# A six-layer cross network on one core: a load put behind another, one split eviction, a changed block order, and single-row-block evictions in the last layer

## The chip, the cores and the metric
The kernel runs on one core of one Trainium2 chip. The metric is the device time of one execution in microseconds (us); lower is better. The core has TensorE (PE) for matmuls into PSUM, VectorE (DVE) and ScalarE (ACT) for elementwise work, GpSimd (POOL), and SyncE (SP), which here only issues DMAs. ACT can issue DMAs too. Sixteen DMA engines serve all queues.

## The reference
Six layers of a cross network over 4096 rows of 416 values (26 x 16), with weights `ws` [6, 416, 416] and biases `bs` [6, 416], all in bf16:

```python
x = x0
for l in range(ws.shape[0]):
    x = x0 * (x @ ws[l] + bs[l]) + x
return x
```

## The kernel before
The activations are held transposed: 416 features are three blocks of 128 (m or k = 0, 1, 2) on the partitions and a remainder of 32. The 4096 rows are columns, in two halves (s = 0, 1) of 2048, each of four column groups (g = 0 to 3) of 512. The three blocks live in `XM` tiles [128, 3, 4096]. The remainder's four groups are packed into 128 partitions, 32 for each g (`XR`); `XRx` is the same with the groups' halves swapped, so that row matmuls of different groups can run side by side in PE's row quarters.

**Loads.** `load_x0t(s, g)` (line 76) is a transposing DMA that brings 512 rows of x0 into `XM[0]`; all eight are issued by SP in the order of g and s. `load_xrem` (line 81) brings the remainder as 64-byte segments, for s = 0 in two parts of 64 partitions (two column groups each); `x0_rem` (line 157) then turns a part into `XR` and `XRx` with three DVE steps: a 32x32 transpose, a reordering copy, and a copy to the swapped place. Line 99 issues the first part on ACT's queue, behind the first layer's weights (line 96), the biases and the remainder's weights. SP issues the transposes for g = 0 to 3 (lines 95, 103 to 105), the second remainder part (106), then the second half's loads and everything else. A DMA waits at its issue until the eighth DMA before it has landed, since there are eight completion semaphores.

**The first layer** (`first_layer`, line 219) goes half by half. For each block m it computes a column pair (two groups, h = 0 or 1) into one pair of PSUM banks; four pairs are used in rotation (`two_banks`, line 131). `full` issues three matmuls (k = 0 to 2) for one (m, group); `row` adds the remainder's product. The order of all this is written out by hand and is PE's order. `ew_main` (line 165) evicts a pair: ACT adds the bias (1 + bias in layer 0, which takes in the "+ x" of that layer) and writes 1024 columns as bf16 into a tile `t`; DVE multiplies by x0 (line 171). A pair can be written again when ACT has read it.

**Layers 1 to 4** (lines 300 to 327) use 32-column tiles of PE for the blocks and evict with two DVE steps, a multiply (line 173) and an add (174). At the end of layer 4, SP issues six transposing DMAs (`xl_dmat`, line 213) that turn the result into rows (`XLrows`).

**The last layer** (line 329 on) has the activations as stationary operand, so its result comes out in rows: 8 "quads" (q) of four 128-row blocks (g), each block 416 wide in one PSUM bank. The first six quads are evicted by pairs (`ew_pair`, line 360): ACT casts 832 columns, DVE multiplies by x0's rows (367) and adds `XLrows` (368), SP stores (369). The last two quads are evicted singly (`ew_single`, line 371): 416 columns each, where the add of a block (`close`, line 379) is issued behind the multiply of the next, so that DVE's neighbouring steps do not depend on each other. `t` tiles come from a pool of 6, output tiles `o` from a pool of 10 of [128, 2, 416].

Of the kernel before, what the change touches and what calls it, by code (L numbers as in the profile page):

```python
# [9 lines left out]
ACT = mybir.ActivationFunctionType  # L10
ALU = mybir.AluOpType
BF16 = mybir.dt.bfloat16
# [4 lines left out]
def kernel(  # L17
# [7 lines left out]
    nc = tc.nc  # L25
    B, D = x0.shape
    L = ws.shape[0]
    P = 128
    NK = 3
# [3 lines left out]
    NG = 4  # L33
    CW = 512
# [6 lines left out]
    tpool = ctx.enter_context(tc.tile_pool(name="tpool", bufs=6))  # L41
    opool = ctx.enter_context(tc.tile_pool(name="opool", bufs=10))
# [27 lines left out]
    def col0(s, g):  # L70
        return SW * s + CW * g
# [4 lines left out]
    def load_x0t(s, g):  # L76
        c0 = col0(s, g)
        nc.sync.dma_start_transpose(out=XM[0][:, :, c0:c0 + CW], in_=x0[c0:c0 + CW, 0:NK * P])  # L78


    def load_xrem(eng, s, p0, p1):
        with nc.allow_non_contiguous_dma(reason="64B row segments"):
            eng.dma_start(xrem[s][p0:p1], x0[SW * s + 16 * p0:SW * s + 16 * p1, NK * P:D].rearrange("(p t) r -> p t r", t=16))
# [12 lines left out]
    load_wm(nc.scalar, 0)  # L96
    nc.scalar.dma_start(bsb[:], bs[:, :])
    load_wr(nc.scalar, 0, 0, 1)
    load_xrem(nc.scalar, 0, 0, 64)
    nc.scalar.activation(dz[:, 1:2], dz[:, 0:1], ACT.Identity, bias=dz[:, 0:1], scale=1.0)  # L100
    for g in range(1, NG):
        nc.vector.tensor_copy(WR[32 * g:32 * g + 32, 0, :], WR[0:32, 0, :])  # L102
    load_x0t(0, 1)
    load_x0t(0, 2)
    load_x0t(0, 3)
    load_xrem(nc.sync, 0, 64, 128)
# [24 lines left out]
    def two_banks():  # L131
        i = 2 * (turn[0] % 4)
        turn[0] += 1
        return PS[:, i:i + 2, :]
# [22 lines left out]
    def x0_rem(s, p0, p1):  # L157
        nc.vector.transpose(out=xrt[s][p0:p1], in_=xrem[s][p0:p1])  # L158
        nc.vector.tensor_copy(XR[0][p0:p1, CW * s:CW * s + CW].rearrange("p (j t) -> p j t", t=16),
                              xrt[s][p0:p1].rearrange("p t j -> p j t"))  # L160
        for a in range(p0, p1, 64):
            nc.vector.tensor_copy(XRx[s][64 - a:128 - a, :], XR[0][a:a + 64, CW * s:CW * s + CW])


    def ew_main(l, s, m, h, pt, cur, nxt):
        c0 = col0(s, 2 * h)
        t = tpool.tile([P, 2 * CW], BF16, name="t")
        nc.scalar.activation(t[:], pt.rearrange("p a b -> p (a b)"), ACT.Identity, bias=bM[:, m, l:l + 1], scale=1.0)  # L168
        x0c = XM[0][:, m, c0:c0 + 2 * CW]
        if l == 0:  # L170
            nc.vector.tensor_tensor(out=nxt[:, m, c0:c0 + 2 * CW], in0=t[:], in1=x0c, op=ALU.mult)  # L171
            return
        nc.vector.tensor_tensor(out=t[:], in0=t[:], in1=x0c, op=ALU.mult)  # L173
        nc.vector.tensor_tensor(out=nxt[:, m, c0:c0 + 2 * CW], in0=t[:], in1=cur[:, m, c0:c0 + 2 * CW], op=ALU.add)  # L174

    def ew_rem(l, s, pr, curR, nxtR):
        tr = tpool.tile([P, 2 * CW], BF16, name="t")
        nc.scalar.activation(tr[:, 0:CW], pr, ACT.Identity, bias=bR[:, l:l + 1], scale=1.0)  # L178
        x0c = XR[0][:, CW * s:CW * s + CW]
        if l == 0:  # L180
            nc.vector.tensor_tensor(out=nxtR[:, CW * s:CW * s + CW], in0=tr[:, 0:CW], in1=x0c, op=ALU.mult)
            return
        nc.vector.tensor_tensor(out=tr[:, 0:CW], in0=tr[:, 0:CW], in1=x0c, op=ALU.mult)
        nc.vector.tensor_tensor(out=nxtR[:, CW * s:CW * s + CW], in0=tr[:, 0:CW], in1=curR[:, CW * s:CW * s + CW], op=ALU.add)
# [34 lines left out]
    def first_layer(s):  # L219
        cur, nxt = XM[0], XM[1]  # L220

        def full(pt, m, h, gl, first, last):
            c0 = col0(s, 2 * h + gl)
            for k in range(NK):
                nc.tensor.matmul(pt[:, gl, :], lhsT=WM[:, 0, k, 128 * m:128 * m + 128], rhs=cur[:, k, c0:c0 + CW],  # L225
                                 start=(first and k == 0), stop=(last and k == NK - 1), skip_group_check=True)

        def row(pt, m, h, swapped, first):
            for gl in range(2):
                r0 = 32 * ((2 * h + gl + 2 * swapped) % 4)  # L230
                src = XRx[s][r0:r0 + 32, :] if swapped else XR[0][r0:r0 + 32, CW * s:CW * s + CW]
                nc.tensor.matmul(pt[:, gl, :], lhsT=WR[r0:r0 + 32, 0, 128 * m:128 * m + 128], rhs=src,  # L232
                                 start=first, stop=(not first), tile_position=(r0, 0), skip_group_check=True)

        pa = [two_banks() for m in range(NK)]
        if s == 0:
            for gl in range(2):
                for m in range(NK):
                    full(pa[m], m, 0, gl, True, False)
        else:  # L240
            for m, gl in ((0, 0), (1, 0), (0, 1), (1, 1), (2, 0), (2, 1)):
                full(pa[m], m, 0, gl, True, False)
        pb = [two_banks()]
        row(pa[0], 0, 0, 0, False)
        row(pa[1], 1, 0, 1, False)
        row(pa[2], 2, 0, 0, False)
        if s == 1:
            row(pb[0], 0, 1, 0, True)
        if s == 0:
            x0_rem(0, 64, 128)  # L250
        for m in range(NK):
            ew_main(0, s, m, 0, pa[m], cur, nxt)
        for gl in range(2):
            full(pb[0], 0, 1, gl, s == 0, s == 1)
        if s == 1:
            ew_main(0, s, 0, 1, pb[0], cur, nxt)
        for m in range(1, NK):
            pb.append(two_banks())
            for gl in range(2):
                full(pb[m], m, 1, gl, True, False)  # L260
        if s == 0:
            row(pb[0], 0, 1, 0, False)
            row(pb[1], 1, 1, 0, False)
            row(pb[2], 2, 1, 1, False)
            x0_rem(1, 0, 128)
            for m in range(NK):
                ew_main(0, s, m, 1, pb[m], cur, nxt)
        else:
            row(pb[1], 1, 1, 0, False)
            row(pb[2], 2, 1, 1, False)  # L270
            rem_first(pb)
# [67 lines left out]
    def mm_q_full(q, py, gs, first):  # L339
        for g in gs:  # L340
            for k in range(NK):
                nc.tensor.matmul(py[g // 2][:, g % 2, 0:D], lhsT=cur[:, k, q_cols(q, g)], rhs=WM[:, l, k, :],  # L342
                                 start=(first and k == 0), stop=((not first) and k == NK - 1), skip_group_check=True)
# [13 lines left out]
                                 rhs=bLr[32 * g:32 * g + 1, :], start=False, stop=(q == begun and g < 2), tile_position=(32 * g, 0),  # L357
                                 skip_group_check=True)

    def ew_pair(q, h, py):  # L360
        s, i = quads[q]
        b0 = 16 * s + 8 * h + i
        t = tpool.tile([P, 2 * CW], BF16, name="t")
        tv = t[:, 0:2 * D].rearrange("p (a d) -> p a d", a=2)
        o = opool.tile([P, 2, D], BF16, name="o")
        nc.scalar.copy(tv, py[h][:, :, 0:D])  # L366
        nc.vector.tensor_tensor(out=tv, in0=tv, in1=X0rows[:, b0:b0 + 5:4, :], op=ALU.mult)  # L367
        nc.vector.tensor_tensor(out=o[:], in0=tv, in1=XLrows[:, b0:b0 + 5:4, :], op=ALU.add)  # L368
        nc.sync.dma_start(out_v[:, b0:b0 + 5:4, :], o[:])

    def ew_single(q, g, py):
        s, i = quads[q]
        b = 16 * s + 4 * g + i
        t = tpool.tile([P, 2 * CW], BF16, name="t")
        o = opool.tile([P, 2, D], BF16, name="o")
        nc.scalar.copy(t[:, 0:D], py[g // 2][:, g % 2, 0:D])  # L376
        nc.vector.tensor_tensor(out=t[:, 0:D], in0=t[:, 0:D], in1=X0rows[:, b, :], op=ALU.mult)  # L377

        def close():
            nc.vector.tensor_tensor(out=o[:, 0, :], in0=t[:, 0:D], in1=XLrows[:, b, :], op=ALU.add)  # L380
            nc.sync.dma_start(out_v[:, b, :], o[:, 0, :])

        return close

    for q in range(0, NQ - 2, 2):
        py = [new_pts()]
        mm_q_full(q, py[0], (0, 1), True)
        py.append(new_pts())
        mm_q_rows((q, q + 1), py, q)
        ew_pair(q, 0, py[0])  # L390
        mm_q_full(q, py[0], (2, 3), False)
        ew_pair(q, 1, py[0])
        for h in range(2):
            mm_q_full(q + 1, py[1], (2 * h, 2 * h + 1), False)
            ew_pair(q + 1, h, py[1])
    pending = []
    for q in range(NQ - 2, NQ):
        py = new_pts()
        mm_q_rows((q,), (py,), None)
        for g in range(NG):  # L400
            mm_q_full(q, py, (g,), False)
            close = ew_single(q, g, py)
            if pending:
                pending.pop()()
            pending.append(close)
    pending.pop()()


# [28 lines left out]
```

## Time and profile before

| | us |
|---|---|
| median of 3 runs | 131.99 (131.69 to 132.15) |
| the profiled execution | 131.1 |
| its span, first to last instruction | 129.3 |
| PE busy | 122.5 (95%) |
| DVE busy | 103.1 (80%) |
| ACT busy | 83.9 (65%) |
| PE waits for a transpose of x0, first layer | 0.4 |
| PE waits for an eviction by ACT, first layer | 0.2 |

Times in the views are counted from the span's start. "Busy" of an engine leaves out its sequencer's work such as issuing DMAs. A matmul's end is modelled and matmuls overlap, so a real gap of PE is longer than the wait that is listed: it is read from the distance of the starts. The 1.8 us of the execution outside the span are taken as fixed. In the timeline a line gives the start, the length, engine, line, operation, the tiles, the shape, the count of merged instructions, and in brackets the idle time before them with what ended it. `SPq` and `ACTq` are those engines' sequencers, here issuing DMAs; `PEld` is PE's weight load.

### The profile page before, as it was taken

What the parts mean: (1) busy time and instruction counts of PE and PEld (TensorE: products, weight loads), DVE (VectorE), ACT (ScalarE), POOL (GpSimd) and SP (SyncE); (2) the same over time, 40 slices, a digit from 0 to 9 for tenths busy, and PEclk for the clock granted to TensorE, in tenths of its full rate; (3) what the DMA queues carried; (4) which work ended last, traced back from release to release, by engine and by line L of the source; (5) the groups of instructions that cost most, each with busy time, mean ns of one, the idle gap of its engine ahead of it and who ended that gap; (6) DMA issues with size and microseconds to landing.
All of it is one profiled execution on the core that took longest, in us unless ns stands there. A gap on an engine that the chain in (4) does not pass through costs nothing.

```text
span 129.3 us, 3927 instructions
## 1 busy us (share of the span) xinstructions
PE 122.5 (95%) x1681; PEld 54.4 (42%) x1683; DVE 103.1 (80%) x186; ACT 83.9 (65%) x92; POOL 5.4 (4%) x18
## 2 busy tenths in 40 slices
PE   6989999999999999999999999999999999999940
PEld 2433343444544444434444544444444345544420
DVE  1163768547989898989898989898989999999990
ACT  0307567598757759756759666849665867567760
POOL 4110000300000000000000000000001200000000
PEclk9999999999999999999999999999999999999997
DMA  3999999999990000000000000000499899996553
GB/s 93 254 213 200 159 182 261 232 329 333 334 298 8 5 0 8 0 0 5 0 5 0 5 0 5 0 5 0 82 126 193 162 138 231 225 312 198 191 172 101
DMA packets 42021, 16.37 MB, mean 127 GB/s; under 512 B 30826, under 2 KB 42004, under 8 KB 42004
## 3 DMA queue, kind: packets, MB, share of 16 engines
q1 hardware_dynamic: 40504, 15.70, 54.5%
q10 hardware_dynamic: 1500, 0.42, 1.7%
q8 instruction: 13, 0.21, 0.7%
q14 instruction: 4, 0.03, 0.1%
HBM read 6.15 MB, written 3.41 MB: 74 GB/s over the span
## 4 chain that ended last, share of the span: by engine, by line
PE 88%; DMA 5%; DVE 1%; ACT 1%; SPq 1%; issue 1%; DVEq 0%
PE PS L190 49%; PE PS L342 12%; PE PS L225 10%; PE PS L196 5%; PE PS L207 5%; DMA XM<-in_x_dram 5%; PE PS L202 2%; PE PS L351 2%; PE PS L232 1%; PE PS L356 1%; SPq L78 1%; DVE t L377 1%; ACT t L168 1%; DVE o L380 1%; ACT t L376 0%
## 5 line engine op out<-in xcount | busy, mean ns | idle before, releaser
L168 ACT ACTIVATE t<-PS,bM 128x1024 bf16<-128x1024 f32 x60 | 62.1, 1114 | 30.8 <-PE PS L196 21.3
L190 PE MATMUL PS<-XM,WM 128*32 128x512 bf16 x1152 | 65.2, 379 | 0.0
L190 PEld LDWEIGHTS <-WM 128*32 128x32 bf16 x1152 | 29.7, 97 | 33.8 <-issue 5.1
L173 DVE TENSOR_TENSOR t<-t,XM 128x1024 bf16<-128x1024 bf16 x48 | 33.3, 694 | 4.2 <-ACT t L168 4.2
L174 DVE TENSOR_TENSOR XM<-t,XM 128x1024 bf16<-128x1024 bf16 x48 | 33.5, 699 | 3.1
L342 PE MATMUL PS<-WM,XM 128*128 128x416 bf16 x96 | 17.9, 340 | 0.0
L225 PE MATMUL PS<-XM,WM 128*128 128x512 bf16 x70 | 16.6, 379 | 0.7 <-DMA XM<-in_x_dram 0.4
L366 ACT CAST t<-PS 128x832 bf16<-128x832 f32 x12 | 10.2, 852 | 5.0 <-PE PS L342 2.5
L342 PEld LDWEIGHTS <-XM 128*128 128x128 bf16 x96 | 8.9, 98 | 8.7 <-issue 2.2
L225 PEld LDWEIGHTS <-WM 128*128 128x128 bf16 x72 | 6.8, 98 | 10.1 <-issue 2.7
L171 DVE TENSOR_TENSOR XM<-t,XM 128x1024 bf16<-128x1024 bf16 x12 | 7.9, 689 | 2.3 <-ACT t L168 2.1
L207 PE MATMUL PS<-XM,WM 128*32 128x512 bf16 x120 | 8.2, 379 | 0.0
L178 ACT ACTIVATE t<-PS,bR 128x512 bf16<-128x512 f32 x10 | 6.8, 694 | 1.4 <-PE PS L207 1.4
L368 DVE TENSOR_TENSOR o<-t,XLrows 128x832 bf16<-128x832 bf16 x12 | 7.1, 592 | 0.5
L196 PE MATMUL PS<-XR,WR 32*128 32x512 bf16 x96 | 7.3, 379 | 0.0
L367 DVE TENSOR_TENSOR t<-t,X0rows 128x832 bf16<-128x832 bf16 x12 | 7.0, 584 | 0.0
L158 DVE STREAM_TRANSPOSE xrt<-xrem 64x512 bf16<-64x512 bf16 (+1 forms) x3 | 2.1, 708 | 5.0 <-DMA xrem<-in_x_dram 5.0
L138 PE MATMUL PS<-warm 128*128 128x512 bf16 (+1 forms) x12 | 4.4, 536 | 1.2 <-DVE warm L89 1.2
L376 ACT CAST t<-PS 128x416 bf16<-128x416 f32 x8 | 4.0, 505 | 1.0 <-PE PS L342 0.8
L207 PEld LDWEIGHTS <-WM 128*32 128x32 bf16 x120 | 3.2, 97 | 3.2
L285 POOL COPY XLrows<-scrR 128x512 bf16<-128x512 bf16 x2 | 1.4, 704 | 74.1 <-DMA scrR<-XR 74.1
L102 DVE COPY WR<-WR 32x416 bf16<-32x416 bf16 x3 | 0.8, 259 | 4.5 <-DMA WR<-in_ws_dram 4.4
(39 smaller groups left out, 42.2 us busy)
## 6 DMA issues: line engine op xcount, KB each, us to landing
X0rows<-in_x_dram SPq DMA_DIRECT2D x4, 832.0 KB, 10.6
out_dram<-o SPq DMA_DIRECT2D x12, 208.0 KB, 2.5
WM<-in_ws_dram SPq DMA_DIRECT2D x5, 312.0 KB
out_dram<-o SPq DMA_DIRECT2D x8, 104.0 KB, 1.8
WR<-in_ws_dram SPq DMA_DIRECT2D x4, 130.0 KB, 5.3
WM<-in_ws_dram ACTq DMA_DIRECT2D x1, 312.0 KB, 3.3
XM<-in_x_dram SPq DMA_TRANSPOSE x8, 4.8
xrem<-in_x_dram SPq DMA_DIRECT2D x1, 128.0 KB
```

The lines of the kernel that those rows point to most:

```text
L168: nc.scalar.activation(t[:], pt.rearrange("p a b -> p (a b)"), ACT.Identity, bias=bM[:, m, l:l + 1], scale=1.0)
L171: nc.vector.tensor_tensor(out=nxt[:, m, c0:c0 + 2 * CW], in0=t[:], in1=x0c, op=ALU.mult)
L173: nc.vector.tensor_tensor(out=t[:], in0=t[:], in1=x0c, op=ALU.mult)
L174: nc.vector.tensor_tensor(out=nxt[:, m, c0:c0 + 2 * CW], in0=t[:], in1=cur[:, m, c0:c0 + 2 * CW], op=ALU.add)
L190: nc.tensor.matmul(pts[g // 2][32 * q:32 * q + 32, g % 2, :], lhsT=WM[:, l, k, 128 * m + 32 * q:128 * m + 32 * q + 32], rhs=cur[:, k, c0:c ...
L196: nc.tensor.matmul(pts[g // 2][:, g % 2, :], lhsT=WR[32 * g:32 * g + 32, l, 128 * m:128 * m + 128], rhs=curR[32 * g:32 * g + 32, CW * s:CW ...
L207: nc.tensor.matmul(pr[32 * g:32 * g + 32, :], lhsT=WM[:, l, k, NK * P:D], rhs=cur[:, k, c0:c0 + CW], start=False, stop=(k == NK - 1), tile ...
L225: nc.tensor.matmul(pt[:, gl, :], lhsT=WM[:, 0, k, 128 * m:128 * m + 128], rhs=cur[:, k, c0:c0 + CW], start=(first and k == 0), stop=(last ...
L342: nc.tensor.matmul(py[g // 2][:, g % 2, 0:D], lhsT=cur[:, k, q_cols(q, g)], rhs=WM[:, l, k, :], start=(first and k == 0), stop=((not first ...
L366: nc.scalar.copy(tv, py[h][:, :, 0:D])
L367: nc.vector.tensor_tensor(out=tv, in0=tv, in1=X0rows[:, b0:b0 + 5:4, :], op=ALU.mult)
L368: nc.vector.tensor_tensor(out=o[:], in0=tv, in1=XLrows[:, b0:b0 + 5:4, :], op=ALU.add)
```

## The change
The first part of the remainder is issued by SP, behind the transpose of the second column group, and no longer by ACT. In the first layer the row matmuls and the evictions of the first column pair go m = 0, 2, 1 in place of 0, 1, 2 (the one that reads `XRx` last); in the second half the blocks of the second column pair go (0,0), (1,0), (0,1), (1,1), (2,0), (2,1), where (m, g) were (0,0), (0,1), (1,0) and so on; one eviction, of m = 0 in the first half's second column pair, is split: ACT takes its first 512 columns and DVE the other 512, in one step that adds the bias and multiplies. In the last layer all 32 blocks are evicted singly, with each add behind the next block's multiply, `o` tiles hold one block (the pool is still of 10), and the very last store is issued by ACT.

```diff
     load_wr(nc.scalar, 0, 0, 1)
-    load_xrem(nc.scalar, 0, 0, 64)
     nc.scalar.activation(dz[:, 1:2], dz[:, 0:1], ACT.Identity, bias=dz[:, 0:1], scale=1.0)
...
     load_x0t(0, 1)
+    load_xrem(nc.sync, 0, 0, 64)
     load_x0t(0, 2)
     load_x0t(0, 3)
...
+    def split_first(s, m, h, pt, nxt):
+        c0 = col0(s, 2 * h)
+        t = tpool.tile([P, 2 * CW], BF16, name="t")
+        nc.scalar.activation(t[:, 0:CW], pt[:, 0, :], ACT.Identity, bias=bM[:, m, 0:1], scale=1.0)
+        nc.vector.scalar_tensor_tensor(out=nxt[:, m, c0 + CW:c0 + 2 * CW], in0=pt[:, 1, :], scalar=bM[:, m, 0:1],
+                                       in1=XM[0][:, m, c0 + CW:c0 + 2 * CW], op0=ALU.add, op1=ALU.mult)
+        nc.vector.tensor_tensor(out=nxt[:, m, c0:c0 + CW], in0=t[:, 0:CW], in1=XM[0][:, m, c0:c0 + CW], op=ALU.mult)
...
         row(pa[0], 0, 0, 0, False)
-        row(pa[1], 1, 0, 1, False)
-        row(pa[2], 2, 0, 0, False)
         if s == 1:
             row(pb[0], 0, 1, 0, True)
+        row(pa[2], 2, 0, 0, False)
+        row(pa[1], 1, 0, 1, False)
         if s == 0:
             x0_rem(0, 64, 128)
-        for m in range(NK):
+        for m in (0, 2, 1):
             ew_main(0, s, m, 0, pa[m], cur, nxt)
-        for gl in range(2):
-            full(pb[0], 0, 1, gl, s == 0, s == 1)
-        if s == 1:
-            ew_main(0, s, 0, 1, pb[0], cur, nxt)
-        for m in range(1, NK):
-            pb.append(two_banks())
-            for gl in range(2):
-                full(pb[m], m, 1, gl, True, False)
+        pb += [two_banks() for m in range(1, NK)]
+        for m, gl in ((0, 0), (0, 1), (1, 0), (1, 1), (2, 0), (2, 1)) if s == 0 else ((0, 0), (1, 0), (0, 1), (1, 1), (2, 0), (2, 1)):
+            full(pb[m], m, 1, gl, s == 0 or m > 0, s == 1 and m == 0)
+            if s == 1 and (m, gl) == (0, 1):
+                ew_main(0, s, 0, 1, pb[0], cur, nxt)
         if s == 0:
...
+            split_first(s, 0, 1, pb[0], nxt)
             x0_rem(1, 0, 128)
-            for m in range(NK):
+            for m in range(1, NK):
                 ew_main(0, s, m, 1, pb[m], cur, nxt)
...
-    def ew_pair(q, h, py):
...
     def ew_single(q, g, py):
...
-        o = opool.tile([P, 2, D], BF16, name="o")
+        o = opool.tile([P, D], BF16, name="o")
...
         def close():
-            nc.vector.tensor_tensor(out=o[:, 0, :], in0=t[:, 0:D], in1=XLrows[:, b, :], op=ALU.add)
-            nc.sync.dma_start(out_v[:, b, :], o[:, 0, :])
+            nc.vector.tensor_tensor(out=o[:], in0=t[:, 0:D], in1=XLrows[:, b, :], op=ALU.add)
+            (nc.scalar if (q, g) == (NQ - 1, NG - 1) else nc.sync).dma_start(out_v[:, b, :], o[:])
...
         mm_q_rows((q, q + 1), py, q)
-        ew_pair(q, 0, py[0])
-        mm_q_full(q, py[0], (2, 3), False)
-        ew_pair(q, 1, py[0])
-        for h in range(2):
-            mm_q_full(q + 1, py[1], (2 * h, 2 * h + 1), False)
-            ew_pair(q + 1, h, py[1])
-    pending = []
+        for g in range(2):
+            evict(q, g, py[0])
+        for a, g in ((0, 2), (0, 3), (1, 0), (1, 1), (1, 2), (1, 3)):
+            mm_q_full(q + a, py[a], (g,), False)
+            evict(q + a, g, py[a])
```

`evict` calls `ew_single` and then the `close` of the block before, as the last two quads' loop did before.

More of the change, by code (lines that the diff above doesn't have):

```diff
@@ L358, in mm_q_rows @@
                                  skip_group_check=True)
-    def ew_pair(q, h, py):
[L361 to L364, printed above, removed]
-        o = opool.tile([P, 2, D], BF16, name="o")
[L366 to L369, printed above, removed]
     def ew_single(q, g, py):
@@ L374, in ew_single @@
         t = tpool.tile([P, 2 * CW], BF16, name="t")
-        o = opool.tile([P, 2, D], BF16, name="o")
+        o = opool.tile([P, D], BF16, name="o")
         nc.scalar.copy(t[:, 0:D], py[g // 2][:, g % 2, 0:D])
@@ L379, in close, with evict @@
         def close():
-            nc.vector.tensor_tensor(out=o[:, 0, :], in0=t[:, 0:D], in1=XLrows[:, b, :], op=ALU.add)
-            nc.sync.dma_start(out_v[:, b, :], o[:, 0, :])
-        return close
+            nc.vector.tensor_tensor(out=o[:], in0=t[:, 0:D], in1=XLrows[:, b, :], op=ALU.add)
+            (nc.scalar if (q, g) == (NQ - 1, NG - 1) else nc.sync).dma_start(out_v[:, b, :], o[:])
+        return close
+    pending = []
+    def evict(q, g, py):
+        close = ew_single(q, g, py)
+        if pending:
+            pending.pop()()
+        pending.append(close)
     for q in range(0, NQ - 2, 2):
@@ L401 @@
             mm_q_full(q, py, (g,), False)
[L402 to L405, printed above, removed]
+            evict(q, g, py)
     pending.pop()()
```

## The prediction
> **What bounds the kernel now.** I read the 40 slices first, then the chain that ended last, then the timeline of the two ends of the span, where the change lies.
>
> The slices of the page, TensorE (PE) and the DMA engines:
> ```profile
> PE   6989999999999999999999999999999999999940
> ...
> DMA  3999999999990000000000000000499899996553
> ```
> A slice is 3.23 us. PE is full from slice 4 (about 10 us) to slice 38 (about 124 us), so time can only be won ahead of that, where PE has gaps and the DMA engines are full, and behind it, in the tail after the last matmul. The chain names the waits at the front (start, length, what):
> ```profile
> 2.17 5.92 DMA XM<-in_x_dram
> 8.09 0.04 issue
> 8.13 2.10 PE PS L225 x9
> ...
> 15.27 1.12 ACT t L168
> 16.40 0.04 issue
> 16.44 3.40 PE PS L225 x15
> ```
> Nine matmuls take 2.10 with a last one of 0.379, so they start 0.215 apart. The nine before these began at 5.64 and could have been followed at 7.58; the second transpose of x0 (call it T2, columns g=1) landed at 8.09 and PE went on at 8.13: 0.55 lost. At 16.44 PE waited for ScalarE (ACT) to free a PSUM pair: the three matmuls before began from 15.38 on, the next was due at 16.03; 0.4 lost. A third, smaller wait is seen only in the weight loads of the timeline:
> ```profile
> 2.27 0.63 ACTq L83 DMA_DIRECT2D xrem<-in_x_dram  x1
> ...
> 7.87 0.70 DVE L158 STREAM_TRANSPOSE xrt<-xrem 64x512 bf16<-64x512 bf16 x1 [0.77 <-DMA xrem<-in_x_dram]
> ...
> 11.51 2.90 PEld L225 LDWEIGHTS <-WM 128*128 128x128 bf16 x14 [0.27 <-issue]
> ...
> 11.92 0.71 DVE L158 STREAM_TRANSPOSE xrt<-xrem 64x512 bf16<-64x512 bf16 x1 [2.41 <-DMA xrem<-in_x_dram]
> ...
> 20.20 4.13 ACT L168 ACTIVATE t<-PS,bM 128x1024 bf16<-128x1024 f32 x4 [1.80 <-PE PS L232]
> 20.31 3.57 PEld L225 LDWEIGHTS <-WM 128*128 128x128 bf16 x18 [0.42 <-issue]
> ```
> The loads are idle 0.12 between neighbours but 0.27 ahead of 11.51: the fourth transpose (T4, issued 6.59, landing 4.88 later, at 11.47) held PE for 0.15. All that the front can give is therefore 0.55 + 0.15 + 0.4 = 1.1 us. The tail:
> ```profile
> 114.38 0.58 DVE L367 TENSOR_TENSOR t<-t,X0rows 128x832 bf16<-128x832 bf16 x1
> 115.00 0.59 DVE L368 TENSOR_TENSOR o<-t,XLrows 128x832 bf16<-128x832 bf16 x1
> 115.51 0.58 DVE L367 TENSOR_TENSOR t<-t,X0rows 128x832 bf16<-128x832 bf16 x1
> ...
> 122.86 2.09 ACT L376 CAST t<-PS 128x416 bf16<-128x416 f32 x4 [0.59 <-PE PS L342]
> ...
> 125.12 0.36 DVE L377 TENSOR_TENSOR t<-t,X0rows 128x416 bf16<-128x416 bf16 x1
> 125.40 0.65 DVE L380 TENSOR_TENSOR o<-t,XLrows 128x416 bf16<-128x416 bf16 x2
> ```
> The last add ends at 126.05; the last store is issued at 126.42, because SP is still busy until 126.33 issuing the store before. It lands at about 128.2 and the span ends at 129.3.
>
> **Part 1, the first remainder part behind T2 on SP.** It leaves ACT's queue, where its 0.63 hid nothing, and becomes SP's third issue. In the stretch 5.5 to 7.0 us the DMA view counts 1040 packets on ACT's queue (q10, 0.07 MB) beside 1170 on SP's (q1), at 47.9% and 88.3% of the sixteen engines. Without them T2 should land about 1.5 x 47.9/136.2 = 0.53 sooner, at about 7.55, and PE's wait of 0.55 goes. The next wait is T4's. PE reaches the row matmuls 0.55 sooner (10.16 to 9.61), needs T4 at 10.15 + 0.65 = 10.8, and T4 has not moved by the engines' work: the same packets must pass before it. So the 0.55 returns at T4, and what counts is T4's landing. Against it stands SP: an issue of 0.59 to 0.68 (rows of L83 on SP) is put ahead of T3 and T4, and every later load is behind it as well. Bounds: +0.7 if that issue counts in full; -0.7 if the mixing of two queues was what held T4 and both waits go. SP's transposes are issued in 1.38 at the shortest and 1.64 and 1.82 for T3 and T4, so most of the 0.68 meets slack, not all; I take **+0.2**. The remainder itself lands behind T2 (the second part landed 0.43 after T4), about 8.0; its three VectorE (DVE) steps took 7.87 to 9.51 = 1.64, so the direct copy is ready at 9.3, the swapped one at 9.65, against rows at 9.61 and (swapped, now last) 9.83. Were it 0.8 later, PE's wait for T4 would still hide it. [...]
>
> **Part 2, the split eviction.** Now the pair read by the second half's m=0 is freed by one ACT step of 1.114 (15.27 to 16.39). After, ACT reads 512 columns (L178: 0.69, to 15.96) and DVE the other 512. DVE is busy until 15.50 with three multiplies. The trace has no such DVE step: bounds are 0.42 (L181, 512 columns from SBUF) and 0.69 (ACT's read of 512 from PSUM); I take 0.69, since it reads fp32 from PSUM. Pair free at 15.54 + 0.69 = 16.23 instead of 16.39: **-0.15**; bounds -0.4 (all of the wait) and 0 (DVE late by another 0.2). DVE's step after it ends by 16.7, ahead of the remainder at 17.31.
>
> **Part 3, the block order.** In the first half nothing is reached: blocks keep their order, and m=1, now evicted third, is free at about 13.2, needed at 13.45. In the second half the order becomes (0,0), (1,0), (0,1)... Block (1,0) of the second column pair writes the PSUM pair that m=0 of the first used (four pairs in rotation). ACT's eviction of it runs 20.20 to 21.31. Before, PE comes there after two blocks, 20.31 + 2 x 0.65 = 21.6: hidden. After, it comes after one, at 20.97, and waits to 21.35: +0.38. Then m=1's eviction is third (20.20 + 3 x 1.0 + 0.1 = 23.32) and PE wants it at 21.35 + 3 x 0.65 = 23.29: +0.07. Sum **+0.45** (0.3 to 0.55; no reason for a gain, as no load was late here). What it buys, a later need of the eighth transpose, is not used: PE did not wait for that one.
>
> **Part 4, single evictions.** Twelve pairs become 24 singles. ACT: 24 x 0.505 - 12 x 0.852 = +1.9 us, beside PE: 8 singles need 4.3 of the 5.15 that PE takes. DVE: a pair starts every 1.13 (114.38 to 115.51), two singles take four starts 0.285 apart = 1.14: equal, +0.15 over the layer at most. DVE begins at 107.56 and 55 starts bring it to 123.26, where now it waits for ACT until 123.40; so nothing passes to the end. Output tiles: ten singles instead of ten pairs; the eleventh add comes at about 113.8, and the first store (issued 110.32 when SP is free of the transposes) landed 3.1 later with twice the bytes: 113.4. SP issues 31 stores of 0.34 to 0.37, one per 0.57. **0** (-0.1 to +0.2).
>
> **Part 5, the last store on ACT's queue.** ACT is idle after 124.95, so the store starts at 126.07 instead of 126.42: **-0.35**. Bounds: ACT's few issues took 0.32 to 0.66, so a slow one leaves 0; -0.45 with the wait trimmed.
>
> **Sum:** +0.2 - 0.15 + 0.45 + 0 - 0.35 = +0.15 on the profiled execution's 131.1 us (span 129.3). That execution lies 0.9 under the median 131.99 of the three timed runs; the difference is added to the median: **132.15 us**.
>
> **Rivals.**
> (a) The two queues held each other up, T4 comes 0.7 sooner, and part 1 is -0.7: sum -0.75, **131.25**. For it: q1's packets were fewest while q10 ran. Against: they were as few at 7.00 to 7.75 (167 GB/s), after q10 had ended.
> (b) Slower: the issue put ahead of T3 counts in full. After the third remainder SP needed 2.90 for the next transpose instead of about 1.4; half as large a part, 0.7. It decides from T4 landing after 11.7: sum +0.65, **132.65**.
> (c) Slower: DVE's fixed cost per instruction. A single lasts 0.368, half a pair's 0.584 is 0.292; only the overlap of neighbours brings the starts to 0.285. With 48 such steps ahead of the tail, a distance above 0.288 uses up the 0.14 of slack; at 0.31, a third of the way to 0.368, the end is 55 x 0.025 - 0.14 = 1.2 later: **133.35**. Against it: eight singles in the trace do keep 0.285. [...]
> (d) The store on ACT gains nothing, its first issue since the start being slow: +0.35, **132.5**.
>
> **Chances.** Forecast 0.41, (a) 0.25, (b) 0.16, (c) 0.07, (d) 0.11. 0.3%, about what a measurement of this kernel can tell, is 0.4 us: faster 0.25, same 0.41, slower 0.34. The range takes in (a), (b), (d): 131.1 to 132.9; the forecast's own is 131.6 to 132.4.
>
> **What would show it.** Right: no PE wait near 7.6, a new one of 0.7 or more ahead of T4's block; ACT still ending PE's wait near 16.3; a new wait of 0.4 one block into the second half's second column pair; DVE starts 0.285 apart; last store issued within 0.1 of the last add. Wrong: T4 landing before 11.0 or after 12.0, or DVE idle for an output tile near 114.

## The result, and the profile after

The changed kernel takes 132.61 us (median of 22 runs, 131.95 to 133.47); the kernel before took 131.93 beside it (22 runs, 131.43 to 132.88). The ratio is 1.0049 [1.0031, 1.0067], +0.65 us: slower by more than 0.3%. The forecast was 132.15, "same", with 131.6 to 132.4 as its own range and 131.1 to 132.9 as the whole one. The time is outside the first and inside the second, and is that of the slower rival (b), 132.65.

The profiled execution of after took 132.79 (span 131.0), near its median. The one of before, 131.1, lies 0.8 below its median and below the fastest of the 22 runs, 131.43. So the two traces stand 1.69 apart where the medians stand 0.68 apart, and not every difference between them belongs to the change.

The slices of after, TensorE and the DMA engines (3.27 us each):
```profile
span 131.0 us, 4011 instructions
...
PE   6998999999999999999999999999999999999920
...
DMA  3999999999992000000000000000597999964665
```
PE's 8 at the front has moved from the third slice, where T2's wait was, to the fourth, where T4's is now; and the loads at the front reach into the thirteenth slice. The timeline of after, SyncE's issues and PE at the front:
```profile
0.73 4.17 SPq L78 DMA_TRANSPOSE XM<-in_x_dram  x2
...
4.95 0.67 SPq L83 DMA_DIRECT2D xrem<-in_x_dram  x1
...
5.67 3.60 SPq L78 DMA_TRANSPOSE XM<-in_x_dram  x2
...
5.86 0.61 PE L138 MATMUL PS<-warm 128*128 128x512 bf16 x1
...
6.25 4.35 PE L234 MATMUL PS<-XM,WM 128*128 128x512 bf16 x18
...
11.08 0.82 PE L234 MATMUL PS<-XM,WM 128*128 128x512 bf16 x3
...
12.23 3.40 PE L234 MATMUL PS<-XM,WM 128*128 128x512 bf16 x15 [0.34 <-DMA XM<-in_x_dram]
```
In before the x18 were two lines of x9 with T2 between them. T2 landed at 6.99 (8.09 before), well ahead of PE. The x18 alone does not show that the change took the wait away, for PE also begins 0.61 later than in before. There the last filler matmul, on a constant tile ahead of the first layer, takes 0.39 and not 0.61:
```profile
5.41 0.39 PE L138 MATMUL PS<-warm 128*128 128x512 bf16 x1
```
Five of the other traces, with the remainder on ACT as before, begin at 6.25 or 6.26 and do not wait for T2 either, though it lands at 7.90 to 8.09. So the 0.55 at T2 that part 1 aims at belongs to executions in which PE begins early, as in the profiled one of before; part 1 alone, below, begins at 5.55 and has no such wait.

Three matmuls last 0.65 by their starts, so the row of 11.08 could have gone on at 11.73; T4, landing at 12.19 (11.47 before), held it to 12.23. That is 0.72 behind before's 11.51.

The next stretch of after: ACT's and DVE's halves of the split eviction, PE, and PE's weight loads in the second half:
```profile
15.98 0.69 ACT L180 ACTIVATE t<-PS,bM 128x512 bf16<-128x512 f32 x1 [1.89 <-PE PS L241]
...
16.10 4.06 PE L234 MATMUL PS<-XM,WM 128*128 128x512 bf16 x18
...
16.63 0.74 DVE L181 SCALAR_TENSOR_TENSOR XM<-PS,bM,XM 128x512 bf16<-128x512 f32 x1
...
21.72 1.82 PEld L234 LDWEIGHTS <-WM 128*128 128x128 bf16 x9 [0.41 <-issue]
...
23.73 0.96 PEld L234 LDWEIGHTS <-WM 128*128 128x128 bf16 x5 [0.19 <-issue]
```
The eighteen matmuls at 16.10 run through: where before PE stood 0.4 for ACT, it stands for nothing, although DVE reads its half until 17.37: the block at 16.75 writes only the bank that ACT has read by 16.67. In the second half the weight loads stop ahead of 21.72 and 23.73, where ACT has just freed a pair: 0.29 and 0.07 of PE. With 0.13 for row matmuls that wait for the remainder, the sum is +0.72 - 0.40 + 0.13 + 0.29 + 0.07 = +0.81; layer 1 begins at 27.18 against 26.36 (0.82). The last layer's first matmul is 0.81 later too, so the layers between hand it on whole.

The tail of after, from the timeline (stores are `SPq` and `ACTq` lines):
```profile
116.94 1.58 SPq L377 DMA_DIRECT2D out_dram<-o  x1
```
```profile
126.26 0.65 DVE L376 TENSOR_TENSOR o<-t,XLrows 128x416 bf16<-128x416 bf16 x2
126.94 0.37 ACTq L377 DMA_DIRECT2D out_dram<-o  x1
```
```profile
126.84 1.87 SPq L377 DMA_DIRECT2D out_dram<-o  x4
...
128.31 0.40 SPq L377 DMA_DIRECT2D out_dram<-o  x1
```
The last add ends at 126.91 and ACT issues its store 0.03 later, as forecast. But SP is behind: three of its stores go out after that one, the last at 128.31, 1.68 after its own add, and it lands last, at 130.05. From last add to last landing it is 3.14, against 2.14 before.

SP's lag also held DVE once, as the chain that ended last shows:
```profile
115.98 3.33 DMA out_dram<-o
...
119.40 0.28 DVE o L376
```
The add at 119.40 waited for an output tile whose store, issued at 115.98, landed at 119.31. DVE started it 0.48 after the step before instead of 0.285, so 0.2 later. In before DVE waits 0.15 for ACT at 123.40; that slack took up most of the 0.2, and the last add comes 0.05 later than the 0.81 by which the last layer begins later.

### The profile page after: what moved, and what is told of

It is laid out like the page before. It is cut to its first block, busy times and chain, and to the rows that moved or that the text cites. A ratio compares the mean times of both kernels' runs of the same rounds, so it can differ in the third digit from the quotient of the medians.

```text
span 131.0 us, 4011 instructions
## 1 busy us (share of the span) xinstructions
PE 123.6 (94%) x1683; PEld 54.7 (42%) x1683; DVE 104.2 (80%) x211; ACT 84.8 (65%) x104; POOL 5.5 (4%) x18
## 5 line engine op out<-in xcount | busy, mean ns | idle before, releaser
L168 ACT ACTIVATE t<-PS,bM 128x1024 bf16<-128x1024 f32 x59 | 61.1, 1114 | 30.3 <-PE PS L205 21.3
L174 DVE TENSOR_TENSOR XM<-t,XM 128x1024 bf16<-128x1024 bf16 x48 | 33.5, 699 | 3.1
L372 ACT CAST t<-PS 128x416 bf16<-128x416 f32 x32 | 15.6, 506 | 4.6 <-PE PS L363 1.8
L376 DVE TENSOR_TENSOR o<-t,XLrows 128x416 bf16<-128x416 bf16 x32 | 11.7, 367 | 0.1
L373 DVE TENSOR_TENSOR t<-t,X0rows 128x416 bf16<-128x416 bf16 x32 | 11.7, 367 | 0.0
L171 DVE TENSOR_TENSOR XM<-t,XM 128x1024 bf16<-128x1024 bf16 x11 | 7.3, 689 | 1.8 <-ACT t L168 1.6
L138 PE MATMUL PS<-warm 128*128 128x512 bf16 (+1 forms) x12 | 5.1, 594 | 1.2 <-DVE warm L89 1.2
L193 DVE TENSOR_TENSOR XR<-t,XR 128x512 bf16<-128x512 bf16 x8 | 3.4, 426 | 0.7
```

Source lines behind the costliest of these rows:

```text
L376: nc.vector.tensor_tensor(out=o[:], in0=t[:, 0:D], in1=XLrows[:, b, :], op=ALU.add)
```

## The experiments

All were timed against the kernel before in five rounds. A time given behind a ratio is the ratio less one, times the median of the kernel before beside it (131.38 to 131.96). The experiments take the parts singly first. Five kept traces have the first layer of before: that of before, those of parts 4 and 5, of part 5 alone and of the joint stores, and that of the last run below. They tell what is chance in it.

**Part 1 alone.**
```diff
-    load_xrem(nc.scalar, 0, 0, 64)
...
     load_x0t(0, 1)
+    load_xrem(nc.sync, 0, 0, 64)
```


> Only part 1: the first remainder part is issued by SP behind the second transpose. Theory (read from the changed kernel's trace): the fourth transpose lands about 0.7 us later and PE waits for it, so +0.7 us (ratio 1.005). Rival, the forecast's step: +0.2. Rival of mixed queues: -0.7. In the profile: the weight load that waits for the fourth transpose begins near 12.2 by the theory, near 11.7 by the forecast, near 10.9 by the third.

Measured: 1.0032 [1.0011, 1.0053], +0.42. PE in its timeline:
```profile
5.55 4.04 PE L225 MATMUL PS<-XM,WM 128*128 128x512 bf16 x18
...
10.06 0.82 PE L225 MATMUL PS<-XM,WM 128*128 128x512 bf16 x3
11.82 3.40 PE L225 MATMUL PS<-XM,WM 128*128 128x512 bf16 x14 [0.94 <-DMA XM<-in_x_dram]
...
16.75 3.40 PE L225 MATMUL PS<-XM,WM 128*128 128x512 bf16 x15 [0.24 <-ACT t L168]
...
21.71 3.40 PE L225 MATMUL PS<-XM,WM 128*128 128x512 bf16 x14 [0.27 <-DMA XM<-in_x_dram]
```
T2's wait is gone, T4's grew to 1.1 (10.71 to 11.82), ACT's stayed, and there is a wait for T8 (the eighth transpose) that the profiled execution of before did not have: T8 landed at 21.67 (20.83 before), 0.4 lost. This second wait cannot be put down to part 1. In the five traces with before's first layer T8 landed at 20.83 to 21.48, and in three of them PE waited for it, 0.14 to 0.58. What T4 costs is clearer. The block behind it begins at 11.66 to 12.23 in the three traces with the load on SP (after, this one, parts 1 to 3), and at 11.30 to 11.89 in the nine traces in which that load, SP's other loads and the block order of the first half are as in before. The means lie 0.37 apart, about what was timed.

**Part 2 alone.**
```diff
+            split_first(s, 0, 1, pb[0], nxt)
             x0_rem(1, 0, 128)
-            for m in range(NK):
+            for m in range(1, NK):
                 ew_main(0, s, m, 1, pb[m], cur, nxt)
```


> Only part 2: the one eviction split over ACT and DVE. Theory: the next block needs only the bank that ACT frees, so the whole wait of 0.4 us near 16.4 goes: -0.4. Rival, the forecast's step: DVE's half, 0.69 long and behind three multiplies, ends the wait, -0.15. In the profile: PE goes on at about 16.03 by the theory, at 16.27 by the forecast.

Measured: 0.9998 [0.9975, 1.0022], 0.0 us. PE in its timeline:
```profile
15.34 4.06 PE L233 MATMUL PS<-XM,WM 128*128 128x512 bf16 x18
...
19.94 0.82 PE L233 MATMUL PS<-XM,WM 128*128 128x512 bf16 x3
21.12 3.40 PE L233 MATMUL PS<-XM,WM 128*128 128x512 bf16 x14 [0.36 <-DMA XM<-in_x_dram]
```
The wait for ACT is gone in full: x18 at 15.34, no break at 16. At 20.59 PE then wants T8, which landed at 21.08: 0.53 lost, more than was won. The transpose that PE "did not wait for" in the profiled execution of before was simply there 0.1 before PE came (20.83 against 20.96); in other executions it is not.

**Part 3 alone.**
```diff
-        row(pa[1], 1, 0, 1, False)
-        row(pa[2], 2, 0, 0, False)
         if s == 1:
             row(pb[0], 0, 1, 0, True)
+        row(pa[2], 2, 0, 0, False)
+        row(pa[1], 1, 0, 1, False)
...
-        for m in range(NK):
+        for m in (0, 2, 1):
...
+        for m, gl in ((0, 0), (0, 1), (1, 0), (1, 1), (2, 0), (2, 1)) if s == 0 else ((0, 0), (1, 0), (0, 1), (1, 1), (2, 0), (2, 1)):
```


> Only part 3: rows and evictions in the order m = 0, 2, 1 and the changed block order of the second half. Theory and forecast agree: +0.45, a wait of 0.38 for ACT ahead of the second block and 0.07 ahead of the fifth. Rival: the rows' order of the first half gives something back, so 0.2 or less.

Measured: 1.0051 [1.0035, 1.0068], +0.67. PE in its timeline:
```profile
10.92 2.76 PE L225 MATMUL PS<-XM,WM 128*128 128x512 bf16 x11
13.99 1.46 PE L225 MATMUL PS<-XM,WM 128*128 128x512 bf16 x6 [0.31 <-ACT t L168]
...
16.97 3.40 PE L225 MATMUL PS<-XM,WM 128*128 128x512 bf16 x15 [0.24 <-ACT t L168]
...
21.90 3.47 PE L225 MATMUL PS<-XM,WM 128*128 128x512 bf16 x14 [0.23 <-ACT t L168]
```
Three waits for ACT. The one at 21.90 is the forecast 0.38 (measured 0.40). The one at 13.99 (0.47) was not forecast: m=1, evicted third, is wanted in the first half too.

**Parts 4 and 5 alone** (the whole last layer of after), and **part 5 alone:**
```diff
-            nc.sync.dma_start(out_v[:, b, :], o[:, 0, :])
+            (nc.scalar if (q, g) == (NQ - 1, NG - 1) else nc.sync).dma_start(out_v[:, b, :], o[:, 0, :])
```


> Only the last layer: all blocks evicted singly, last store on ACT. Theory: SP, which starts late behind the transposes and issues a store each 0.49 us, does not catch up with an add each 0.57, so its last store goes out 1 us or more after the add: +0.3 to +1.0. Rival, the forecast's step: SP catches up and the last store on ACT gives -0.35. In the profile: the last SP store starts within 0.3 of its add by the rival, over 0.8 behind it by the theory.

> Only part 5: the very last store issued by ACT, the last layer still in pairs but for its last two quads. Theory and forecast: the store starts at its add instead of 0.37 later, -0.35. Rival: a first issue on ACT after so long is slow, 0.

Measured: parts 4 and 5 1.0003 [0.998, 1.0026], 0.0; part 5 1.002 [1.0003, 1.0037], +0.26. The tail of part 5 alone, and the wait for its landing:
```profile
125.62 0.65 DVE L380 TENSOR_TENSOR o<-t,XLrows 128x416 bf16<-128x416 bf16 x2
126.31 0.38 ACTq L381 DMA_DIRECT2D out_dram<-o  x1
```
```profile
SPq L432 <- DMA out_dram<-o: 1.9, 1, 1.9
```
The add ends at 126.28 and the store is issued 0.03 later, 0.12 behind SP's store of the block before. It landed at 128.43, 2.12 after its issue, where in before the last store took 1.77. From add to landing it is 2.15 against 2.14: what the issue gains, the transfer loses. SP waits 1.9 for the landing, against 1.4 in before.

**Pairs stored jointly in the last layer of after,** one store for two blocks in the first six quads (19 issues on SP rather than 31):
```diff
+            if q >= NQ - 2:
+                (nc.scalar if (q, g) == (NQ - 1, NG - 1) else nc.sync).dma_start(out_v[:, b, :], o[:, 0, :])
+            elif e:
+                nc.sync.dma_start(out_v[:, b - 4:b + 1:4, :], o[:])
```


> Parts 4 and 5, but the 24 blocks of the first six quads, still evicted singly, are stored two by two, so that SP issues 19 stores and not 31. Parts 4 and 5 alone gave 0.0. Theory: what took the gain of part 5 is SP's queue of stores, so here SP keeps up and -0.35 is left. Rival: single evictions cost DVE or ACT what part 5 gains, so 0.0 as before.

Measured: 1.0000 [0.9977, 1.0023]. In its trace SP is no longer behind at the end (its last store goes out at 126.52, ahead of the last add's end at 126.61); in that of parts 4 and 5 it is:
```profile
125.28 1.85 SPq L370 DMA_DIRECT2D out_dram<-o  x4
126.14 0.41 ACTq L370 DMA_DIRECT2D out_dram<-o  x1
```
SP's last store goes out at 126.74, 0.9 after its own add (125.82). Taking SP's lag away changes nothing that the timing can tell: the lag is real, and its price in the usual execution lies within the interval, some 0.3 us.

**Parts 1 to 3** with before's last layer:


> Parts 1, 2 and 3 with the last layer as before. Alone they gave +0.4, 0.0 and +0.7. Theory: they overlap. Part 1 brings the rows of the first half forward and so hides m=1's third eviction (0.47 of part 3), and part 3 hides the wait for the eighth transpose that ate part 2's gain; so +0.5 to +0.7, all of the change's +0.65. Rival: the parts add up to +1.1, and the last layer gives 0.4 back.

Measured: 1.0035 [1.0017, 1.0054], +0.46, which with the last layer's 0.0 agrees with the whole change's +0.65 [0.41, 0.88] within the intervals. PE in its timeline:
```profile
11.66 3.46 PE L233 MATMUL PS<-XM,WM 128*128 128x512 bf16 x15 [0.25 <-DMA XM<-in_x_dram]
...
15.58 4.06 PE L233 MATMUL PS<-XM,WM 128*128 128x512 bf16 x18
...
20.44 4.41 PE L233 MATMUL PS<-XM,WM 128*128 128x512 bf16 x18
```
The 0.47 of part 3 in the first half is down to 0.06: x15 lasts 3.46 where 3.40 is free of waits, because ACT begins earlier (the row matmuls start at 10.05 here, at 10.38 in part 3 alone) while PE, held 0.4 by T4 (11.24 to 11.66), comes to that pair no earlier. The second-half wait for ACT stays, hidden in a merged line (4.41 against 4.06, 0.35).

**The order without its wait.** If part 3's loss is the pair that ACT frees too late, splitting that eviction as well should leave the gain: T8 is needed one block later, and ACT frees the first bank in 0.69 instead of 1.11. No load is moved; rows and evictions keep 0, 1, 2.
```diff
         for m in range(NK):
-            ew_main(0, s, m, 0, pa[m], cur, nxt)
+            if (s, m) == (1, 0):
+                split_first(s, m, 0, pa[m], nxt)
+            else:
+                ew_main(0, s, m, 0, pa[m], cur, nxt)
```
This with part 2, the second half's block order, and part 5; then the same without part 5; then with a third split (first half, m = 0, first pair) and the new block order in both halves:


> A version that should beat both: before, with part 2, part 5, the changed block order of the second half alone (rows and evictions still in the order m = 0, 1, 2), and a second split eviction, of m=0 in the second half's first column pair. Theory: the block that part 3 made wait needs only one bank, which ACT's half frees at 0.69 instead of 1.11, so the wait of 0.38 goes, the eighth transpose is needed later, and both waits of 0.4 are saved: -0.4 - 0.35 = -0.75. Rival: DVE's steps come later for it and the next wait takes most of it: -0.35, part 5 alone.

> The version with two split evictions, without part 5. Part 5 alone gave +0.26, since its store shares the DMA engines with the one issued 0.12 before it and lands 2.15 after its add, as it did on SP (2.14). Theory: this version, -0.37 with part 5, comes to -0.4 to -0.6. Rival: part 5's +0.26 was chance, so -0.37 as before.

> As the version with two splits without part 5, and the first half gets the same block order, with a third split (m=0 of its first column pair, DVE's half ahead of the second remainder part). Theory: the fourth transpose is needed 0.65 later, so its wait of 0.15 to 0.4 goes as well: another -0.2 to -0.35, -0.6 to -0.9 in all. Rival: the next wait (the eighth transpose, landing 20.5 to 21.5) takes it, no gain over two splits.

Measured: 0.9972 [0.9956, 0.9988], -0.37; without part 5 0.9966 [0.9945, 0.9987], -0.45; three splits 0.9966 [0.9940, 0.9992], -0.45. PE of the second of them:
```profile
10.60 4.10 PE L233 MATMUL PS<-XM,WM 128*128 128x512 bf16 x17
...
15.16 4.06 PE L233 MATMUL PS<-XM,WM 128*128 128x512 bf16 x18
19.41 0.39 PE L240 MATMUL PS<-XR,WR 32*128 32x512 bf16 x2 [0.18 <-DVE XR L159]
...
20.27 4.16 PE L233 MATMUL PS<-XM,WM 128*128 128x512 bf16 x17
```
Eighteen without a break last 4.06, so the second half's first column pair loses nothing to ACT and its second one 0.1, to T8 (landing at 21.63). This kernel beats before, by 0.17 to 0.73, and so after. What it still loses lies ahead of 20.27: PE starts the row matmuls late and breaks off between them, since DVE's steps on the second half's remainder come late; from the last matmul at 18.84 to 20.27 it is 1.42, where 0.85 is free of waits, so 0.57 lost. With three splits PE does not wait for T4, but T4 landed at 10.76 there, so it would not have waited with the old order either: that run does not test the third split. It lost 0.27 to the remainder and 0.19 to T8 (21.67). The loads are the limit in both.

**A small load in the remainder's place.** For the last two runs two theories were on record: A, that an issue put ahead of T3 and T4 on SP makes all later transposes late; B, that the remainder's packets, not its issue, set their landing. Is it SP's issue or the remainder's 64-byte packets that delays T4? One of the last layer's bias rows, 832 bytes, goes behind T2:
```diff
     load_x0t(0, 1)
+    nc.sync.dma_start(bLr[0:1, :], bs[LL:LL + 1, :])
     load_x0t(0, 2)
```


> Before, with one of the four bias loads of 832 bytes (issue 0.25) moved ahead of the third transpose on SP, where part 1 put the remainder. Theory A, an issue in front of them delays all later transposes: the eighth lands 0.3 or more later than its 20.5 to 21.5, the fourth 0.2 later, and the time grows by 0.1 to 0.3. Theory B, part 1's cost is the moving of its 1024 packets of 64 bytes behind the second transpose: landings as before, 0.0.

Measured: 1.0015 [0.9996, 1.0034], +0.20. In its trace T4 landed at 11.78 and T8 at 22.67, as late as with the remainder there or later; but that execution, 132.91, was the slowest of its twelve. It leans to A and does not settle it.

**The remainder later on ACT,** to take its packets out of T2's way without SP:
```diff
-    load_xrem(nc.scalar, 0, 0, 64)
     nc.scalar.activation(dz[:, 1:2], dz[:, 0:1], ACT.Identity, bias=dz[:, 0:1], scale=1.0)
+    load_xrem(nc.scalar, 0, 0, 64)
```


> Before, with the first remainder part still on ACT's queue but issued behind the activation-table load and the first activation, at about 3.9 instead of 2.27. By theory A the fourth and the eighth transpose land as before (11.4 and 20.9) and the second one may land near 7.0, so -0.3 to 0.0. By theory B, if the packets go behind the second transpose, the fourth and eighth land later as in part 1 (11.8 and 21.7): +0.4.

Measured: 0.9990 [0.9968, 1.0012]. The edit moved no load: ACT's sequencer issued it at 2.36 (2.27 before), while the activation written ahead of it began at 3.58. So it does not test the theories, but it is a second trace of before's loads, in an execution of 131.71, nearer to the usual one. PE in it:
```profile
6.08 4.11 PE L225 MATMUL PS<-XM,WM 128*128 128x512 bf16 x18
...
21.52 3.40 PE L225 MATMUL PS<-XM,WM 128*128 128x512 bf16 x14 [0.42 <-DMA XM<-in_x_dram]
```
The waits for T2 (0.07) and T4 (none) are all but gone by themselves, and PE waits 0.58 for T8 (landing at 21.48). Layer 1 begins at 26.91, 0.55 later than in the profiled execution of before. The waits that the prediction was built on were those of one execution, faster than any of the 22 timed beside after.

## Why the prediction was right in its range and wrong in its steps

The time lies in the whole range because rivals were priced in it. That it meets rival (b), 132.65, within 0.04 is luck: (b) prices part 1 at 0.7, which alone measured 0.42, and keeps part 5's gain of 0.35, which did not come. The steps, one by one:

**Part 1: the direction was right, and the size may have been (+0.2; alone +0.42 [0.14, 0.70]).** T2's wait went and came back at T4, as said. T2 came 1.1 sooner, not 0.53 (6.78 to 6.99 in three traces with the load on SP, 7.90 to 8.09 in ten without), which bought nothing. T4 came 0.6 later in the mean: 11.61 to 12.19 in the three, 10.76 to 11.54 in the ten without any added issue. It was issued about 1.0 later (7.47 to 7.78 against 6.41 to 6.71), so part of that delay did meet slack, as the prediction has it. And the step ended with T4. "Every later load is behind it as well" was written and not followed to T8, which landed at 21.67, 21.77 and 22.26 against 20.49 to 21.67, 0.8 later in the mean. That "T4 has not moved by the engines' work: the same packets must pass before it" was the author's estimate and was not shown; the issue put ahead of T3 and T4 takes 0.67 on SP. Rival (b), deciding "from T4 landing after 11.7", is what came in after (12.19) and in part 1 alone (11.78).

**Part 2: the step "DVE's half frees the pair at 16.23" failed.** DVE's half took 0.745 and ended at 17.37, later than allowed, and it cost nothing: the next block writes only the first bank, which ACT's 0.69 frees. So the full 0.4 of that wait went, the lower bound. But part 2 alone gave 0.0 (interval -0.3 to +0.3, so the -0.15 itself is not excluded), and its trace shows where the gain went: PE came to T8 at 20.59 and waited 0.53. The prediction said where the 0.55 of T2 goes and not where this 0.15 goes.

**Part 3: +0.45, alone +0.67 [0.46, 0.89].** The two second-half waits came as worked out: 0.40 and 0.07 alone, 0.29 and 0.07 in the whole. "In the first half nothing is reached" holds only with part 1 (0.06 in parts 1 to 3); alone it is 0.47. And "what it buys, a later need of the eighth transpose, is not used" was true of the profiled execution and not of the kernel: PE waited for T8 in three of the five traces with before's first layer, and in those of part 1 and part 2 alone. The new order covers that. In after no wait for T8 is left, though it lands at 22.26.

**The sum.** The parts alone make 0.42 - 0.03 + 0.67 + 0.04 = 1.1; together they make 0.65, and parts 1 to 3 make 0.46 where singly they make 1.06, which is just outside what the intervals allow. The traces show the overlap: with part 1 the wait for T4 takes the place of part 3's first-half wait, and part 3 covers T8. Separate terms may be added only where the next limit is far.

**Part 4: a total of 0 fits what was timed; one of its reasons failed.** Part 4 was not run alone; parts 4 and 5 together gave 0.0 and part 5 alone +0.26, each with 0.2 to 0.3 either way. DVE's starts are 0.285 apart, no output tile held it near 114 (one did at 119.40, for 0.2), rival (c) did not come. "SP issues 31 stores of 0.34 to 0.37, one per 0.57" took lengths of stores that SP issues when idle. Queued, they take 0.39 to 0.40 and start 0.49 apart, one took 1.58, and the first went out at 111.94 rather than 110.32: 0.8 of this is the later first layer, and 0.8 is the issue of the last of the six transposes, 3.13 against 2.31. The first add ended at 109.30, so SP began 2.6 behind, and at 0.57 - 0.49 = 0.08 won per store 31 stores do not make that up. That gave the profiled execution a tail 1.0 longer; that it costs the usual one anything, no timing shows. In the trace of parts 4 and 5 SP began only 1.5 behind and would have made that up, but there too one store took 1.5 to issue.

**Part 5: -0.35 failed.** The store left 0.03 after the add, and gained nothing (+0.26 alone, interval 0.04 to 0.49; without it the two splits are no slower). Why it should lose a quarter of a microsecond is not shown: the add-to-landing time grew by 0.01 in its trace, and by 0.2 in that of the two splits (2.35 against 2.14). Rival (d) had the outcome and the wrong cause: the issue was quick (0.38). Two stores 0.12 apart are in flight together, and each took longer to land than in before: the one ahead 2.05 from its issue (1.83 in before), the last one 2.12 (1.77). That the one holds up the other was not shown apart from that. The prediction reckoned with the packets of two queues side by side in part 1 and not here.

So +0.15 became +0.65: part 5's 0.35 is missing, part 1 is some 0.2 dearer (within its interval), and the rest of the differences nearly cancel.

What stays open: how much of T4's and T8's delay is SP's issue slot and how much the remainder's packets, as the run meant to tell these apart leans one way only and the other moved nothing.

## What to carry to other kernels

Ask of every wait that a change removes which wait stands behind it, and how far: here T4 stood behind T2, and T8 behind ACT's wait, so no single part gained, while two splits with the later need of T8 gained 0.4 together. Before such a wait is priced, see whether it is there in a second trace: of ten traces with the loads as before, five have no wait for T2 at all, and T8 was waited for in three of five, though not in the one that was read. When an issue is put into a queue that bounds a stage, follow its delay to the end of that queue: here T4 and T8 both landed later. Moving the last store to an idle queue saved its issue time and lost it again in flight (2.12 from issue to landing, 1.77 in before), with the store ahead of it not yet landed.

## What the runs showed of the hardware that was not expected

- A block waited only for the bank it writes: an eviction split over two engines freed the first bank in 0.69 us instead of 1.11. With part 2 alone PE wrote that bank from 15.99 on, while DVE read the other until 16.50 (0.745 in all).
- In the last run a DMA written behind an activation in ACT's program was issued ahead of it: at 2.36 us, with the activation at 3.58. Written ahead of it, in before, it was issued at 2.27.
- With the loads unchanged in order, T8 landed anywhere between 20.49 and 21.67 us in ten traces, and the first matmul of layer 0 began between 5.62 and 6.26: differences of 0.1 between single traces say nothing at this end of the kernel. Matmuls of 512 columns lasted 0.63 us at first and 0.38 later, and the change came early in the trace of before (the filler at 4.83 us lasts 0.38) and late in that of after (the matmul at 6.25 us still lasts 0.63).
- Stores of 104 KB that stood in SP's queue in after were issued 0.49 us apart (eight starts from 113.53 to 116.94).
